# A table of attention decays written with one transfer and without its rows of ones, and its steps placed anew in a planned order

## The chip, the core and the metric

One core of a Trainium2 chip runs the whole program. Times are device microseconds of one execution. The core has five engines that run their own instruction lists side by side: PE (TensorE; its weight loads are listed apart as PEld), DVE (VectorE), ACT (ScalarE), POOL (GpSimd) and SP (SyncE, which here issues nearly every transfer between DRAM and the core's memory). An engine takes its instructions strictly in the order of its list, and an instruction waits until the steps that it needs have ended.

## The reference

Three stages follow each other: causal attention whose scores carry a decay, then two MLPs on the 2304 tokens (4 batches of 576) of width 512.

```python
# q, k, v: (4, 8, 576, 64), s: (4, 8, 576)
cum = np.cumsum(np.maximum(s, 0.0), axis=-1)
bias = -(cum[:, :, :, None] - cum[:, :, None, :])
scores = np.matmul(q, k.transpose(0, 1, 3, 2)) / np.sqrt(D)
scores = np.where(causal, -1e9, scores + np.minimum(bias, 0.0))
attn = softmax(scores)                       # + 1e-9 in the sum
x = (attn @ v) as 2304 tokens x 512
g = s1 * np.maximum(x @ w_in, 0.0) ** 2 + b1     # w_in 512 x 2048
x = g @ w_out                                # w_out 2048 x 512
h = np.maximum(np.maximum(x @ w1, x @ w2), x @ w3)   # 512 x 768 each
return h @ w_out2                            # 768 x 512
```

The bias at query i and key j is `cum[j] - cum[i]`. Only its part that depends on the key has to stand in the scores (what depends on the query alone leaves the softmax as it is), and the kernel takes off a middle value of the query's chunk to keep the numbers small.

## The kernel before

**Jobs.** Attention runs in jobs of two heads of one batch. The four pairs of batch 0 are split into an A job (queries 0 to 319) and a B job (queries 320 to 575) each: jobs 0 to 7. The twelve pairs of the other batches are one W job each: jobs 8 to 19. For each job PE makes the scores in units of up to 128 queries (`qk` L521/L523, `qk_set` L531 for W jobs), DVE adds the mask and takes the row's least value (`least` L542), ACT takes the exponentials into `pp` (`expo` L548), PE transposes `pp` into a bank `pt` (`turn_p` L589), ACT or DVE copies the bank into the job's buffer `pt` (`copy_p`, which is recorded under `copy`, L235 on ACT and L239 on DVE), and PE multiplies with v (`av` L608). Beside that DVE inverts the rows' sums (`inverse` L555/L556), POOL splits them into two parts (`rr`, L562/L563), PE turns and spreads them (L567, L579), and DVE multiplies the job's result with them (`x`, L613), which is split into `xhi` and `xlo` and stored (L625).

**Two ways to the decay.** For jobs 0 to 7 PE multiplies a one-hot tile `oh` (L511) with the tile `dd`, five pieces that hold the decays of every head as a rounded part and a rest: `df` is the decay (DVE), `dh` its rounding (ACT, L498), `dd` the rounding or the rest (DVE, L502). For the W jobs the scores of one head are made from two static tiles `set` [128, 4, 576] whose slots are QA, KA (rounded q and k over what is left of them) and KB, QB (the same crosswise). In rows 0 to 63 of KB and QB stand zeros but for rows 0 to 3: two rows of decays against rows of ones, in KB rows 0 and 1 are decays and 2 and 3 ones, in QB the other way round. So one product over all 128 rows adds the decay to the score. `clear_set` zeroes those rows once (POOL memset, L449), `round_set` (ACT, L471) and `rest_set` (POOL, recorded in `minus`, L242) fill the rest for each head, and `decay_set` brings the four rows of the head (L481).

**The table.** Those rows come from a table of all 32 heads in DRAM, `dm_d`. It is made in `dm` [32, 4, 576]: row 0 is the rounded `cum` (ACT, L430), row 1 what is left (DVE, L432), rows 2 and 3 the middle values of the chunks (DVE, L435/L437). `save_d` (L439 to L442) writes it with four transfers: two of `dm` and two that spread the constant `ones`, so that `dm_d` has for each head two blocks of four rows, one for KB and one for QB.

**What shares memory.** `dm` lies in the buffer of the second static set. `s4`, which holds `cum`, `ones` and `dh`, and `df` lie in buffers of the later `pt` tiles: the half-size `pt` of jobs 0 to 3 are cut out of the same two. So the first `copy_p` of a job must not start before the last `dd` is made, and before the change not before the table is saved either:

```python
over += [("dd", NC - 1), ("save_d",)]        # L766
```

**The weights.** Meanwhile a part of the first MLP's weights, `wa_in` and `wa_out`, is converted from a wider format in 16 pieces of 128x512, 8 of `w_in` and 8 of `w_out` (the rest follows in smaller side pieces): a load by SP (L271), a step on ACT (L275), four to six on DVE (L278 to L286), a rounding copy on ACT or DVE (L235, L239), a subtraction and an addition on DVE or POOL (L242, L290). The buffers `wg`, `stage` and `wst` hold a piece on its way. Two of these buffers are the `pt` buffers of the first W jobs: the first `copy_p` of a W job waits until all pieces are through (L765).

**The order.** The steps of this first half are not written in order. Each is handed to a planner with `add(name, engine, cost, priority, needs, ...)`; a step may name two engines with a cost for each. The planner (class `Plan`) simulates the engines by those costs: it takes the step that can begin first, and of steps within 0.03 of that the one with the lowest priority number, and in the order in which it has taken them they are written into the program. So a changed cost, priority or need can move any step on any engine. SP's transfers are ordered by it too.

Of the kernel before, what the change touches and what calls it, by code (L numbers as in the profile page):

```python
# [8 lines left out]
F32 = mybir.dt.float32  # L9
# [24 lines left out]
SET_AT = -10.0  # L34
# [159 lines left out]
def fused_kernel(ctx, tc, q, k, v, s, w_in, w_out, ms, mb, w1, w2, w3, w_fin, out,  # L194
                 f_split=8):
    nc = tc.nc
    B, H, S = s.shape
# [8 lines left out]
    NC = (S + P - 1) // P  # L206
# [118 lines left out]
    NH = B * H  # L325
# [95 lines left out]
    QA, KA, KB, QB = range(4)  # L421
    made = {}
    dm = atp.tile([NH, 4, S], F32R, name="dm", tag="set1")
    dmf = dm.bitcast(F32)
    dm_d = dram.tile([NH, 2, 4, S], F32, name="dm_d")

# [12 lines left out]
    def save_d():  # L439
        for z in range(2):  # L440
            nc.sync.dma_start(dm_d[:, z, 2 * z:2 * z + 2], dmf[:, 2 * z:2 * z + 2])
            nc.sync.dma_start(dm_d[:, 1 - z, 2 * z:2 * z + 2], ones[:NH].unsqueeze(1).to_broadcast([NH, 2, S]))  # L442

# [3 lines left out]
    def clear_set(z):  # L447
        made[z] = atp.tile([P, 4, S], F32R, name="set", tag=f"set{z}")
        nc.gpsimd.memset(made[z][:D, KB:].bitcast(F32), 0.0)  # L449

    def load_sb():
# [28 lines left out]
    def decay_set(job, j):  # L480
        nc.sync.dma_start(hs_[job.n, j][0:4, KB:].bitcast(F32), dm_d[2 * job.p + j].rearrange("t r n -> r t n"))  # L481

# [202 lines left out]
    for x, e in enumerate(("ACT", "DVE", "DVE", "DVE")):  # L685
        add(("dm", x), e, act(S) if e == "ACT" else dve(S), 8.0 + x, [("pre", "DVE")] + [("dm", y) for y in range(x)], decays, x, att=True)
    add(("save_d",), "SP", (4, 16), 8.0, [("dm", x) for x in range(4)], save_d, att=True)
    for z in range(2):
        add(("set", z), "Pool", 0.9, 20.0, [("save_d",)], clear_set, z, att=True)
    jobs = [Job(n, n % NP, "AB"[n // NP]) if n < 2 * NP else Job(n, n - NP, "W") for n in range((B + 1) * NP)]  # L690
    t0 = 0.0
    qk_key = lambda n, u, j: ("qk", n, u) if n < 2 * NP else ("qk", n, u, j)
    for job in jobs:
# [18 lines left out]
        if pairs:  # L712
            for key, when, m in (("q", Q_LOAD, job.q1 - job.q0), ("k", K_LOAD, job.keys)):
                add((key, n), "SP", (2, m), t0 + when, [] if key == "q" else [("q", n)], load_qk, job, key, take=[("raw", [("qk", n, u) for u in units])] if key == "q" else [], **a)
            add(("oh", n), "Pool", 0.3, t0 + TURN, [("qk", n - 2, u) for u in range(6)], one_hot, job, **a)
        else:
            for j in range(2):
                th = t0 + j * period / 2
                add(("q", n, j), "SP", (2, 2 * S), th + Q_LOAD, [], load_both, job, j, take=[("raw", [("rest", n, j), ("again", n, j)])], **a)
                add(("round", n, j), "ACT", act(2 * S), th + SET_AT, [("q", n, j)] + [("set", z) for z in range(2)], round_set, job, j, take=[("hs", [("qk", n, u, j) for u in units])], **a)  # L720
                add(("decay", n, j), "SP", (2, 16), th + SET_AT + 1, [("round", n, j), ("save_d",)], decay_set, job, j, **a)
                add(("rest", n, j), "Pool", pool_(2 * S), th + SET_AT + 1, [("round", n, j)], rest_set, job, j, **a)
                add(("again", n, j), {"Pool": pool_norm(S), "ACT": act(S)}, 0, th + SET_AT + 1.5, [("round", n, j)], again_set, job, j, **a)
# [30 lines left out]
        for z, (u, j) in enumerate(turns):  # L754
# [8 lines left out]
                if x == 0:  # L763
                    over = [("after", ("copy_p", n - 1, jobs[n - 1].units[-1], j))] if n else []
                    if 2 * NP <= n < 2 * NP + 3:  # L765
                        over += [("w", "a", z, 8) for z in range(16)] + [("av", 2 * NP - 1 - z, g) for z in range(2) for g in jobs[2 * NP - 1].groups]  # L766
                    over += [("dd", NC - 1), ("save_d",)]
                    take = [("ph" if n < 2 * NP else "p", [("av", n, g) for g in job.groups])]
# [428 lines left out]
```

## Time and profile before

| | |
|---|---|
| timed runs | 936.35, 941.95, 943.08 us; median 941.95 |
| profiled execution | 936.99 us, its span 935.2 us, mean granted clock of PE 0.991 |
| PE busy | 904.8 us (97% of the span), 5872 instructions |
| DVE busy | 518.1 us (55%) |
| ACT busy | 448.0 us (48%) |
| POOL busy | 243.9 us (26%) |

The span is the time that the profile shows; the execution's own time has a little more around it. A share over the whole span is a mean over stages with different limits: the attention and the first MLP overlap in the first third or so, the second MLP takes the rest. So the table says that PE fills the end, and nothing of what sets the start; for that the stretches have to be read apart.

In the rows further down, "out<-in" are the program's names, a size like 128x320 is partitions by elements, "x4" is a number of instructions, and brackets at the end of a row give the idle time of the engine just before it and what ended it. L12 is line 12 of the kernel before. In the new program some lines stand one further up or down (L548 is L549 there, L498 is L499, L449 is L447 and L448, L625 is L626).

### The profile page before, as it was taken

The numbers are of one execution on the slowest core, as the hardware profiler recorded it, in microseconds if no ns is written. First come the engines' busy times: TensorE is split into PE (matmuls) and PEld (weight loads), VectorE is DVE, ScalarE is ACT, GpSimd is POOL, SyncE is SP. The second block draws the span as 40 slices with busy tenths as digits, with TensorE's granted clock in tenths as the row PEclk, the third lists the DMA queues.
The fourth block names the chain that finished last, engine by engine and source line by source line (L and its number), as shares of the span: only waits on it lengthen the run. The fifth ranks groups of instructions, "written<-read, shape, count | busy, mean of one in ns | idle before, by whom it ended". The sixth has DMA issues, their size and how long they took to land.

```text
span 935.2 us, 16309 instructions
## 1 busy us (share of the span) xinstructions
PE 904.8 (97%) x5872; PEld 850.8 (91%) x5872; DVE 518.1 (55%) x1327; ACT 448.0 (48%) x1158; POOL 243.9 (26%) x286
## 2 busy tenths in 40 slices
PE   4899899999999999999999999999999999999997
PEld 3677789988898999999999999999999999999997
DVE  8798978877887312226687578578521213121221
ACT  4788699999977623324344335334221212121111
POOL 3344457655644233223233123210000000000000
PEclk8799999999999999999999999999999999999999
DMA  7455466675654003803334333433110202010000
GB/s 231 149 154 187 147 198 190 202 229 166 193 183 147 20 29 127 316 29 124 119 91 129 120 101 127 144 119 105 51 66 1 68 1 68 1 51 1 23 12 34
DMA packets 72497, 104.11 MB, mean 111 GB/s; under 512 B 7392, under 2 KB 48096, under 8 KB 72416
## 3 DMA queue, kind: packets, MB, share of 16 engines
q1 hardware_dynamic: 72320, 102.92, 34.9%
q8 instruction: 46, 0.75, 0.3%
q14 instruction: 35, 0.29, 0.1%
q10 hardware_dynamic: 96, 0.15, 0.0%
HBM read 75.19 MB, written 27.85 MB: 110 GB/s over the span
## 4 chain that ended last, share of the span: by engine, by line
PE 82%; DMA 6%; DVE 5%; ACT 4%; SPq 2%; issue 1%; POOL 1%; POOLq 0%; ACTq 0%; DVEq 0%
PE mm L246 23%; PE mm L248 23%; PE mm L247 23%; PE pt L589 4%; PE px L608 4%; PE ps L531 3%; PE ps L521 1%; DMA xs<-x_d 1%; DMA stage<-in_moe_w_in_dram 1%; DVE pp L542 1%; DMA raw<-in_k_dram 1%; ACT pt L235 1%; PE pr L579 1%; POOL ga L242 1%; DMA wb_in<-wb_d 1%
## 5 line engine op out<-in xcount | busy, mean ns | idle before, releaser
L246 PE MATMUL mm<-yh,wt 128*128 128x384 f32 x432 | 146.4, 339 | 0.0
L248 PE MATMUL mm<-yh,wt 128*128 128x384 f32 x432 | 146.3, 339 | 0.0
L247 PE MATMUL mm<-yl,wt 128*128 128x384 f32 x432 | 146.3, 339 | 0.0
L1101 DVE TENSOR_TENSOR u<-mm,u 128x384 f32<-128x384 f32 x72 | 40.1, 556 | 185.2 <-PE mm L248 185.2
L965 ACT ACTIVATE g<-g 128x384 f32<-128x384 f32 (+2 forms) x112 | 53.5, 477 | 146.1 <-DVE g L961 145.9
L589 PE MATMUL pt<-ident,pp 128*128 128x128 f32 x480 | 79.0, 280 | 15.9 <-ACT pt L235 12.5
L548 ACT ACTIVATE pp<-pp,mn 128x192 f32<-128x192 f32 (+4 forms) x160 | 88.8, 559 | 2.7 <-DVE mn L542 2.5
L242 POOL TENSOR_TENSOR gbl<-g,gbh 128x384 fp32r<-128x384 f32 x48 | 51.1, 1065 | 145.2 <-ACT gbh L235 134.5
L1105 ACT ACTIVATE hh<-u 128x384 fp32r<-128x384 f32 x36 | 18.9, 525 | 134.7 <-DVE u L1101 134.7
L246 PEld LDWEIGHTS mm<-yh,wt 128*128 128x128 f32 x432 | 81.2, 188 | 1.3
L247 PEld LDWEIGHTS mm<-yl,wt 128*128 128x128 f32 x432 | 81.2, 188 | 1.3
L248 PEld LDWEIGHTS mm<-yh,wt 128*128 128x128 f32 x432 | 81.2, 188 | 0.0
L242 POOL TENSOR_TENSOR set<-raw,set 64x1152 fp32r<-64x1152 f32 x24 | 65.1, 2712 | 61.4 <-ACT set L471 55.9
L246 PE MATMUL mm<-xhi,wa_in 128*128 128x320 f32 (+1 forms) x256 | 79.8, 312 | 1.3 <-DVE ya L1016 1.3
L961 DVE TENSOR_SCALAR g<-mm 128x384 f32<-128x384 f32 (+2 forms) x112 | 55.4, 495 | 45.0 <-PE mm L248 38.8
L246 PE MATMUL mm<-ga,wa_out 128*128 128x320 f32 (+2 forms) x256 | 79.8, 312 | 0.1
L248 PE MATMUL mm<-ga,wa_out 128*128 128x320 f32 (+2 forms) x256 | 76.2, 298 | 2.7 <-DVE wa_out L290 2.7
L589 PEld LDWEIGHTS pt<-ident,pp 128*128 128x128 f32 x480 | 56.1, 142 | 24.7 <-ACT pt L235 14.3
L235 ACT ACTIVATE pt<-pt 128x256 f32<-128x256 f32 (+3 forms) x181 | 72.4, 427 | 10.8 <-PE pt L589 8.9
L247 PE MATMUL mm<-ga,wa_out 128*128 128x320 f32 (+2 forms) x256 | 76.1, 297 | 0.8 <-POOL ga L242 0.8
L242 POOL TENSOR_TENSOR ga<-g,ga 128x320 fp32r<-128x320 f32 (+1 forms) x64 | 54.0, 845 | 87.4 <-ACT ga L235 85.2
L247 PE MATMUL mm<-xlo,wa_in 128*128 128x320 f32 (+1 forms) x256 | 75.8, 296 | 0.2 <-POOL xlo L242 0.2
(170 smaller groups left out, 2290.7 us busy)
## 6 DMA issues: line engine op xcount, KB each, us to landing
wst<-in_moe_w_dram SPq DMA_DIRECT2D x24, 384.0 KB, 3.7
raw<-in_q_dram SPq DMA_DIRECT2D x24, 288.0 KB, 3.6
raw<-in_k_dram SPq DMA_DIRECT2D x24, 288.0 KB, 3.8
wb_d<-wbs SPq DMA_DIRECT2D x21, 256.0 KB, 3.0
xs<-x_d SPq DMA_DIRECT2D x24, 192.0 KB, 3.7
y<-y_d SPq DMA_DIRECT2D x24, 192.0 KB
y_d<-y SPq DMA_DIRECT2D x24, 192.0 KB
yt<-y_d SPq DMA_DIRECT2D x24, 192.0 KB, 2.8
```

The source lines that it names most:

```text
L235: nc.scalar.activation(dst, src, AF.Copy, scale=1.0 if scale is None else scale)
L242: ENGINES[on].tensor_tensor(dst, a, b, op=ALU.subtract)
L246: nc.tensor.matmul(ps, lhs[0], rhs[0], start=first, stop=False)
L247: nc.tensor.matmul(ps, lhs[0], rhs[1], start=False, stop=False)
L248: nc.tensor.matmul(ps, lhs[1], rhs[0], start=False, stop=last)
L531: nc.tensor.matmul(ps[:, :k1 - k0], t[:, a, QS[i]:QS[i] + P], t[:, b, k0:k1], start=x == 0, stop=x == 1)
L548: nc.scalar.activation(p[:n, :w], p[:n, :w], AF.Exp, bias=mns[job.n, j][:n, i:i + 1], scale=-1.0, accum_out=sums[job.n % 2][:n, j, i:i + 1])
L589: nc.tensor.transpose(pt[:, c - c0, :], pp[j][i][:, c * P:(c + 1) * P], ident)
L608: nc.tensor.matmul(px_[job.n][hf][j * D:(j + 1) * D, a0 - h0:h1 - h0], vn[job.n % 2][:, c, j, :], columns(job, pr["p", job.n, j], c, c + 1 ...
L961: nc.vector.tensor_scalar(st["g", f], st["u", f][:, :n], 0.0, None, op0=ALU.max)
L965: nc.scalar.activation(st["g", f], st["g", f], AF.Square)
L1101: nc.vector.tensor_tensor(us[t0, f], us[t0, f, i][:, :N3], us[t0, f], op=ALU.max)
```

## The change

The table in DRAM holds four rows for each head and no ones; one transfer writes it. `clear_set` now sets rows 0 to 3 of KB and QB to one (a second memset on POOL), and `decay_set` brings two rows into KB (rows 0 and 1) and two into QB (rows 2 and 3) by two transfers for each head in place of one; the rows of ones are never written again. In the plan, the table's first two steps get an earlier place and its last two a later one, the save a later one, costs are fitted to the new steps, and the first `copy_p` of a job needs the second step of the table (the last that reads `cum`) in place of the save.

```diff
-    dm_d = dram.tile([NH, 2, 4, S], F32, name="dm_d")
+    dm_d = dram.tile([NH, 4, S], F32, name="dm_d")
...
     def save_d():
-        for z in range(2):
-            nc.sync.dma_start(dm_d[:, z, 2 * z:2 * z + 2], dmf[:, 2 * z:2 * z + 2])
-            nc.sync.dma_start(dm_d[:, 1 - z, 2 * z:2 * z + 2], ones[:NH].unsqueeze(1).to_broadcast([NH, 2, S]))
+        nc.sync.dma_start(dm_d, dmf)
...
     def clear_set(z):
         made[z] = atp.tile([P, 4, S], F32R, name="set", tag=f"set{z}")
         nc.gpsimd.memset(made[z][:D, KB:].bitcast(F32), 0.0)
+        nc.gpsimd.memset(made[z][:4, KB:].bitcast(F32), 1.0)
...
     def decay_set(job, j):
-        nc.sync.dma_start(hs_[job.n, j][0:4, KB:].bitcast(F32), dm_d[2 * job.p + j].rearrange("t r n -> r t n"))
+        t = hs_[job.n, j].bitcast(F32)
+        for a, z in ((0, KB), (2, QB)):
+            nc.sync.dma_start(t[a:a + 2, z], dm_d[2 * job.p + j, a:a + 2])
...
     for x, e in enumerate(("ACT", "DVE", "DVE", "DVE")):
-        add(("dm", x), e, act(S) if e == "ACT" else dve(S), 8.0 + x, [("pre", "DVE")] + [("dm", y) for y in range(x)], decays, x, att=True)
-    add(("save_d",), "SP", (4, 16), 8.0, [("dm", x) for x in range(4)], save_d, att=True)
+        add(("dm", x), e, act(S) if e == "ACT" else dve(S), (-1.0 if x < 2 else 12.0) + x, [("pre", "DVE")] + [("dm", y) for y in range(x)], decays, x, att=True)
+    add(("save_d",), "SP", (1, 72), 14.0, [("dm", x) for x in range(4)], save_d, att=True)
     for z in range(2):
-        add(("set", z), "Pool", 0.9, 20.0, [("save_d",)], clear_set, z, att=True)
+        add(("set", z), "Pool", 2.2, 20.0, [("save_d",)], clear_set, z, att=True)
...
-                add(("decay", n, j), "SP", (2, 16), th + SET_AT + 1, [("round", n, j), ("save_d",)], decay_set, job, j, **a)
+                add(("decay", n, j), "SP", (2, 18), th + SET_AT + 1, [("round", n, j), ("save_d",)], decay_set, job, j, **a)
...
-                    over += [("dd", NC - 1), ("save_d",)]
+                    over += [("dd", NC - 1), ("dm", 1)]
```

The plan comes out anew on all engines. Three places of it matter here.

ACT, from the last of the decays' roundings (`s_110<-df 128x576`, the `dh` that the last `dd` needs; its tile is named after the memory) to the first copies `pt` of job 0. Before:

```order
L498 ACTIVATE s_110<-df 128x576
L548 ACTIVATE pp_1_151,sums_144<-pp_1_151,mn 128x192
L548 ACTIVATE pp_1_156,sums_144<-pp_1_156,mn 128x192
L548 ACTIVATE pp_2_152,sums_144<-pp_2_152,mn 128x320
L275 ACTIVATE wg<-wg 128x512 x2
L548 ACTIVATE pp_2_157,sums_144<-pp_2_157,mn 128x320
L275 ACTIVATE stage<-stage 128x512 x2
L235 ACTIVATE wa_in<-wg 128x512
L275 ACTIVATE stage<-wst 128x512
L275 ACTIVATE wg<-wg 128x512
L235 ACTIVATE wa_in<-wg 128x512
L235 ACTIVATE wa_in<-stage 128x512 x2
```

Behind the last of these rows come the two copies `pt<-pt 128x64`. Now, with what each waits for (a number behind an engine's name is of no matter here, DMAHW7 is the landing of a transfer):

```order
L499 ACTIVATE s_110<-df 128x448 [waits DVE_49,Activation_49]
L275 ACTIVATE wg<-wg 128x512 [waits DMAHW7_49]
L549 ACTIVATE pp_0_150,sums_144<-pp_0_150,mn 64x64 [waits DVE_49]
L549 ACTIVATE pp_0_155,sums_144<-pp_0_155,mn 64x64 [waits DVE_49]
L499 ACTIVATE s_110<-df 128x576 [waits DVE_49]
L549 ACTIVATE pp_1_151,sums_144<-pp_1_151,mn 128x192 [waits DVE_49]
L549 ACTIVATE pp_1_156,sums_144<-pp_1_156,mn 128x192 [waits DVE_49]
L235 ACTIVATE wa_in<-wg 128x512 [waits DVE_49]
L235 ACTIVATE pt<-pt 128x64 [waits DVE_49,PE_49]
L235 ACTIVATE pt<-pt 128x64 [waits PE_49]
L549 ACTIVATE pp_2_152,sums_144<-pp_2_152,mn 128x320
```

The first copy now stands behind four exponentials, one rounding and one step of a weight piece (the second piece, `wg`), which itself has moved ahead of the exponentials; before, six exponentials, six weight steps and four roundings stood ahead of it.

POOL, around the memsets of the static sets. Before, both stood together, ahead of `xlo` of job 0:

```order
L449 MEMSET set 64x1152 x2
L242 TENSOR_TENSOR stage<-stage,wa_in 128x512
L511 CAST oh<-rows 128x128
L290 TENSOR_TENSOR wa_in<-stage 128x512
L242 TENSOR_TENSOR xlo<-x_0_457,xhi 128x320
L562 CAST rr<-rs 128x2x3
```

Now (DMAHW5 is the save of the table):

```order
L242 TENSOR_TENSOR xlo<-x_0_417,xhi 128x320 [waits Activation_49]
L512 CAST oh<-rows 128x128 [waits PE_49]
L447 MEMSET set 64x1152
L448 MEMSET set 4x1152 [waits Pool_49]
L242 TENSOR_TENSOR xlo<-x_0_542,xhi 128x320 [waits Activation_49]
L447 MEMSET set 64x1152 [waits DMAHW5_49]
L448 MEMSET set 4x1152 [waits Pool_49]
L563 CAST rr<-rs 128x2x3 [waits DVE_49]
L564 TENSOR_TENSOR rr<-rs,rr 128x2x3 [waits Pool_49]
```

The memsets have moved behind `xlo` of job 0, the second of them stands behind the save and ahead of `rr` of job 2, and the subtraction and the addition of a `stage` piece have left POOL (three others of the conversion leave it later, all for DVE).

SP, where the weights of `w_out` (`stage<-in_moe_w_out_dram`) and the table's save stand among the attention's loads. Before, from the save on:

```order
L441 DMA dm_d<-dm 32x1152
L442 DMA dm_d<-s_110 32x2x576
L271 DMA wg<-in_moe_w_in_dram 128x512
L487 DMA vn_115<-in_v_dram 128x2x128
L489 DMA vn_115<-in_v_dram 64x128
L461 DMA raw<-in_q_dram 64x320 x2
L271 DMA stage<-in_moe_w_out_dram 128x512 x2
L625 DMA x_d<-x_0_457 128x320
```

Now the save stands behind the result of job 0 (`x_d<-x_0_417`), and the first load of `w_out` further down, behind the keys of job 5:

```order
L626 DMA x_d<-x_0_417 128x320 [waits DMAHW4_49,DVE_49]
L440 DMA dm_d<-dm 32x2304 [waits DMAHW5_49,DVE_49,Activation_49]
L488 DMA vn_116<-in_v_dram 128x2x128 [waits DMAHW6_49,PE_49]
...
L460 DMA raw<-in_k_dram 64x576 [waits DMAHW1_49]
L460 DMA raw<-in_k_dram 64x576 [waits DMAHW2_49]
L271 DMA stage<-in_moe_w_out_dram 128x512 [waits DMAHW3_49,DVE_49]
L488 DMA vn_116<-in_v_dram 128x4x128 [waits DMAHW4_49,PE_49,Pool_49]
```

So the loads of `w_out` come later among the attention's own loads: the second stands behind the next job's q and k, the third behind the first q and k of a W job.

## Rows read from the trace of the kernel before

**Rows 1.** Windows: start:end length, busy of PE PEld DVE ACT POOL, PEclk, DMA, GB/s.

```profile
10.50:34.00 23.50, 9.35 (x47) 6.06 (x48) 19.57 (x55) 13.62 (x39) 5.99 (x6) 0.64 0.66 206
34.00:55.00 21.00, 20.81 (x158) 14.87 (x157) 19.83 (x67) 19.57 (x69) 8.29 (x14) 1.00 0.53 160
55.00:107.20 52.20, 49.22 (x362) 39.44 (x361) 47.11 (x121) 40.59 (x99) 24.17 (x27) 1.00 0.58 175
107.20:266.00 158.80, 156.79 (x1257) 142.06 (x1257) 127.27 (x459) 151.78 (x451) 94.73 (x92) 1.00 0.62 191
...
366.00:935.20 569.20, 563.33 (x3223) 549.35 (x3221) 249.70 (x476) 162.87 (x346) 66.56 (x72) 1.00 0.25 82
```

**Rows 2.** Timeline of PE: start us, length us, line, operation [idle before <-releaser].

```profile
27.07 1.54 PE L589 MATMUL pt<-ident,pp 128*128 128x128 f32 x6 [11.76 <-ACT pt L235]
```

**Rows 3.** Timeline of ACT.

```profile
11.42 0.33 ACT L548 ACTIVATE pp<-pp,mn 64x64 f32<-64x64 f32 x1
...
13.54 0.55 ACT L548 ACTIVATE pp<-pp,mn 128x320 f32<-128x320 f32 x1
14.08 0.65 ACT L275 ACTIVATE wg<-wg 128x512 f32<-128x512 f32 x1
...
26.82 0.85 ACT L235 ACTIVATE pt<-pt 128x64 f32<-128x64 f32 x4
...
107.21 1.37 ACT L235 ACTIVATE pt<-pt 128x64 f32<-128x64 f32 x4 [0.68 <-DVE wa_out L290]
```

**Rows 4.** Timeline of DVE.

```profile
12.94 0.80 DVE L502 SCALAR_TENSOR_TENSOR dd<-s,lower,df 128x576 fp32r<-128x576 f32 x1
...
29.42 0.21 DVE L542 CUSTOM_DVE_ANT_0 pp<-late_keys,ps 64x64 f32<-64x64 f32 x1 [2.83 <-PE ps L523]
...
36.02 0.49 DVE L613 TENSOR_TENSOR x<-px,rb 128x320 f32<-128x320 f32 x1
...
105.89 1.29 DVE L290 TENSOR_TENSOR wa_out<-stage 128x512 fp32r<-128x512 f32 x2
```

**Rows 5.** DVE's groups, 30 to 108 us: operation xcount | busy us, mean ns | idle.

```profile
L239 DVE COPY pt<-pt 128x512 f32<-128x512 f32 x2 | 1.4, 688 | 0.6 <-PE pt L589 0.6
L242 DVE TENSOR_TENSOR wg<-wg,wa_in 128x512 f32<-128x512 f32 x2 | 1.4, 677 | 0.0
...
L239 DVE CAST rt<-pr 128x128 fp32r<-128x128 f32 x2 | 0.6, 288 | 0.9 <-PE pr L567 0.9
```

**Rows 6.** An issue on SP; transfers (KB, us to landing); two rows of POOL.

```profile
8.36 0.58 SPq L271 DMA_DIRECT2D wg<-in_moe_w_in_dram  x1
...
raw<-in_q_dram SPq DMA_DIRECT2D x8, 80.0 KB, 2.4
...
wst<-in_moe_w_dram SPq DMA_DIRECT2D x24, 384.0 KB, 3.7
...
dm_d<-dm SPq DMA_DIRECT2D x2, 144.0 KB, 6.0
...
25.85 1.05 POOL L449 MEMSET set<- 64x1152 f32 x1 [6.30 <-DVE wg L286]
...
43.13 0.19 POOL L562 CAST rr<-rs 128x6 fp32r<-128x6 f32 x1 [2.83 <-DVE rs L556]
```

**Rows 7.** The set loads (ns min/median/max, first to last start) and POOL's first `rest`.

```profile
L481 SPq DMA_DIRECT2D set<-dm_d x24: 268/319/467, 81.4 to 301.7; - x24
...
82.51 3.13 POOL L242 TENSOR_TENSOR set<-raw,set 64x1152 fp32r<-64x1152 f32 x1 [0.34 <-POOL ga L242]
```

**Rows 8.** Timeline of SP's transfer issues: start us, length us.

```profile
36.83 0.99 SPq L271 DMA_DIRECT2D stage<-in_moe_w_out_dram  x2
...
49.00 1.89 SPq L461 DMA_DIRECT2D raw<-in_k_dram  x2
...
76.72 0.42 SPq L467 DMA_DIRECT2D raw<-in_k_dram  x1
...
96.08 0.34 SPq L271 DMA_DIRECT2D stage<-in_moe_w_out_dram  x1
```

## Prediction

> **What bounds the kernel now.** I read the stretches first, then PE's waits, then ACT and DVE in the first 40 us, then the place where the attention's first half hands over to its second.
>
> The stretches [rows 1] show three regimes. From 366 us to the end PE is busy 563.33 of 569.20 us: whatever happens earlier reaches the end only as a shift of that block. From 107.2 to 266 us ACT is busy 151.78 of 158.80 us and is the bound; DVE (127.27) follows. Before 107.2 us DVE is the fullest: 19.83 of 21.00 us, then 47.11 of 52.20. The hole lies between 10.5 and 34 us: of 23.50 us PE fills 9.35, ACT 13.62, but DVE 19.57. Counted on ACT the hole is 9.88 us, counted on DVE only 3.93.
>
> PE's longest wait is 11.76 us, ended at 27.07 by ACT's copies `pt`, which begin at 26.82 [rows 2, 3]. Their inputs had long been there; the plan puts them behind the save of the table, and so behind ACT's steps on weight pieces that land late.
>
> The handover: the first `pt` copy of a W job starts at 107.21, after 0.68 us of waiting for DVE's last `wa_out` additions (105.89 and 1.29 us for two) [rows 3, 4]. It goes into a buffer in which weight pieces were converted, so no W copy can start before the sixteen pieces are through. DVE's work up to there is the clock of the front part, and how much of the 11 us survives it is what has to be predicted.
>
> **The start, moved.** In the new order ACT's first `pt` copy stands behind four exponentials, the first step of weight piece 2 and a rounding of piece 1. Piece 2 is issued at 8.36 and takes 0.58 to issue [rows 6]; ACT runs its step at 14.08 without a wait [rows 3]. The landing is not shown: not after 14.08, and not before 8.94 + 2.4, the quickest median of a load [rows 6]. I take 8.94 + 3.7, that of weight pieces, the nearest row: 12.6. Then 0.6 for the step, 2.1 for the exponentials with `dh` between (11.42 to 13.54 now) and as much for the rounding, which has the step's shape, as for the step [rows 3] put the copy at 15.9, **10.9 us** before 26.82. That is the gain if nothing else were late. DVE is late next. Up to the handover, on DVE:
>
> 1. The wait of 2.83 us at 29.42, for scores behind the copies [rows 4], goes. New: `dd` needs `dh`, which now stands behind piece 2. `dd` starts 1.5 us after the first exponential now (12.94 and 11.42) [rows 3, 4], so at 13.2 + 1.5 = 14.7 in the new order; what stands ahead of it on DVE is what stands there now but for one longer conversion step, so I let it end at 13.2, a little after 12.94. So 1.5 us of waiting come. **-1.3** (-2.8 if the piece lands at 11.3, 0 if at 14.1).
> 2. Five additions of the conversion leave POOL for DVE at 0.68 each: +3.4. In return DVE gives ACT two large `pt` copies of 0.69 and two `rt` copies of 0.29: -2.0 [rows 5]. ACT takes them where it is busy 40.59 of 52.20 us [rows 1], so they cost nothing there; without that cover 2.0. **+1.4** (0.4, if DVE gains 1 us by less disturbance from POOL, to 3.4).
> 3. The second `set` memset on POOL now waits for the table's one save, since the table lies in that set's buffer. Behind it on POOL stands `rr` of job 2, and behind what needs that, on PE's queue, the scores of job 4. `x` of job 0 comes at 36.02 now, so at 25 [rows 4]; the table's last step stands some 4 us of DVE work behind it (sixteen rows of the new order, at 0.2 to 0.5 us each [rows 4]), so the save goes out at about 29. It has 288 KB: 3.7 us as a weight piece, 6.0 as half the table took [rows 6], so it lands between 32.7 and 35. Two memsets follow: 1.05 us [rows 6], and the four-row one, which the trace does not show; the nearest row is again 1.05 (as long, fewer rows), the other bound 0.2. POOL is through between 34 and 37; `rr` is wanted at 43.13 - 10.9 = 32.2 [rows 6]. The stall is 2 to 5 us, but DVE meets it only when the conversions that stand ahead of job 4's scores run out: **+1.0** (0 to 5).
> 4. Between 55 and 107.2 us DVE waits 5.09 us. With the attention ahead of it there is work at hand more often; I let the share fall to that of 34 to 55 us (1.17 of 21.00), so 2.9 of 52.2: **-2.2** [rows 1] (-5.1 to +2).
> 5. `x` of job 7 and two side pieces come ahead of the handover and cost before it what they save behind: 0, within 1 us.
>
> Sum: -1.3 + 1.4 + 1.0 - 2.2 = -1.1 us at the handover. Behind it the same work stands on a saturated ACT, so the shift is carried to the end.
>
> **The rest of the edit.** Four saves become one, off any path. Each of 24 set loads becomes two: one more SP issue of 0.32 us, 7.7 us in all between 81 and 302 us [rows 7]. The cover: SP issued the first at 81.4, and POOL's `rest` on that set, which the scores need as well, ran from 82.51 to 85.64 [rows 7]; a part that lands half a microsecond later stays hidden. Taken as 0; without the cover 7.7. The Trainium skill, page "DMA: Bandwidth & Descriptors", section "Rules for kernel authors", asks to coalesce many small transfers into a large one, since below 64 KB one pays mostly overhead. This part of the edit goes against that; by the rule the sum would be worse by the uncovered price. The trace has borne it out in issue time alone.
>
> The sum is made against the profiled execution, 936.99 us (span 935.2): 935.9. The median of the three timed runs is 941.95, 5.0 us above it, within 936.35 to 943.08; on its scale the sum gives 940.8. A new median may lie anywhere between the two: **938**.
>
> **Rivals.**
> - *The whole hole counts.* If DVE packs its weight work between attention steps and its waits vanish, the shift is the 10.9 us of the first copy: 926 us (928.5 on the middle scale). For it: ACT, the bound from 107 us on, loses 9.88 us in the hole. Against: DVE loses 3.93 there and gets five additions more. Chance 0.17.
> - *Slower: the second half of the weights comes too late.* The eight `wa_out` loads go out between 36.83 and 96.08 [rows 8], and the last additions end at 107.18: 70 us for eight. In the new order the first load stands behind the keys of job 5 (49.00 now [rows 8], so about 38 to 40) and the third behind the first keys of a W job (76.72 now, so about 66). If the chain of load, ACT and DVE for a piece sets the pace and not DVE's work, the handover comes at 111 to 115, 4 to 8 us later: 941 to 945 us (943.5 to 947.5). It decides when the last six pieces take over 41 us from 66. Against: the last load went out at 96.08 and its piece was through 11 us later, side by side with another, so pieces overlap. Chance 0.15.
> - *The start is not freed*, because the copies wait for something of the table after all: 937 (939.5). Against: the first copy's waits in the new order name DVE and PE and no transfer. Chance 0.03.
> - *Set loads uncovered*: 935.9 + 7.7 = 943.6 (946). Chance 0.04.
>
> The forecast's own case has 0.61; its items reach from 929 to 945 together, 931 to 942 if not all fall on one side. The range that leaves out no more than 2 in 10 is **927 to 945**. 1% is 9.4 us, about what a measurement of this kernel can tell from no change. Faster by that needs nearly the whole of the first rival, slower more than the second's price: faster 0.14, same 0.80, slower 0.06.
>
> **What would show it.** The first `pt` copy at 15 to 17 us and no PE wait over 4 us after it. DVE busy about 1.5 us longer before the first W copy, its waits 2 to 4 us shorter, and that copy at 104 to 108. A wait of POOL for the save ahead of the second memset, with `rr` of job 2 behind it. ACT 95% busy from there for some 159 us. If the first W copy comes before 100 us, the first rival holds and items 2 to 4 are too dear; after 110, the second; if it comes at 106 and the end is elsewhere, the carrying behind the handover is wrong.

## The result, and the profile after

The changed kernel takes **947.68 us** (median of 12 executions, 943.77 to 949.82) against 941.89 (936.12 to 944.06) for the kernel before beside it: a ratio of **1.0064**, 95% interval 1.0041 to 1.0087. It is slower by 5.8 us where 938 was forecast and 927 to 945 was the range. The profiled execution took 948.05 us (span 946.2) against 936.99 (935.2), so the two traces lie 11 us apart, more than the medians: the profiled execution of before is one of its shortest.

The stretches of the changed kernel, cut as in [rows 1] but for the third, which again ends at the first `pt` copy of a W job:

```profile
10.50:34.00 23.50, 19.71 (x111) 13.18 (x108) 18.13 (x64) 18.50 (x63) 2.88 (x7) 0.71 0.73 216
34.00:55.00 21.00, 19.84 (x139) 13.85 (x138) 17.08 (x55) 17.48 (x54) 10.09 (x15) 1.00 0.49 143
55.00:115.90 60.90, 49.01 (x323) 38.17 (x322) 53.09 (x127) 40.82 (x100) 20.56 (x25) 0.87 0.48 148
115.90:266.00 150.10, 146.13 (x1169) 130.95 (x1169) 122.68 (x422) 137.78 (x410) 88.39 (x87) 1.00 0.60 187
366.00:946.20 580.20, 574.57 (x3319) 560.76 (x3317) 250.91 (x483) 169.52 (x362) 73.61 (x82) 1.00 0.25 81
```

From 10.5 us to that copy DVE is busy 88.30 of 105.4 us (before 86.51 of 96.7). Its work grew by 1.8 us, its waits by 6.9, and the two make up the 8.7 us by which the copy is late. The waits are the clear part of it: another execution of the kernel before (e14, copy at 107.20) has 88.91 us of DVE's work and 7.79 of waits, so that the work varies within one kernel by more than 1.8 us. Against [rows 1] the waits grew in each of the three stretches: 3.93 to 5.37, 1.17 to 3.92, 5.09 to 7.81. The hole of PE is filled (19.71 for 9.35 us), and another has opened behind 55 us. ACT in the timeline, the first copy of job 0, the last step before the first W copy that waited long, and that copy:

```profile
16.16 0.31 ACT L235 ACTIVATE pt<-pt 128x64 f32<-128x64 f32 x2
...
113.75 0.44 ACT L275 ACTIVATE wb<-wb 128x256 f32<-128x256 f32 x1 [2.35 <-DMA wb<-in_moe_w_in_dram]
...
115.88 1.33 ACT L235 ACTIVATE pt<-pt 128x64 f32<-128x64 f32 x4
```

So the start came as computed (15.9 forecast, 16.16 measured, 26.82 before [rows 3]) and the lead of 10.7 us has turned into a delay of 8.7. The last exponential of a job, read from ACT's timeline, shows where it went:

| last exponential ends, us | job 1 | job 3 | job 4 | job 6 | job 7 |
|---|---|---|---|---|---|
| before | 37.0 | 50.2 | 58.0 | 78.5 | 90.1 |
| changed | 27.1 | 41.0 | 52.9 | 77.2 | 92.8 |

The lead is down to 1.3 us at job 6 and lost at job 7, and all that time the weights are behind: the fifth piece's last addition comes at 54.58 instead of 35.52, the eleventh at 98.19 instead of 73.23. SP's loads of `w_out` and the first side piece behind them, then DVE where it waited or was held up:

```profile
71.50 0.38 SPq L271 DMA_DIRECT2D wst<-in_moe_w_out_dram  x1
...
99.31 0.54 SPq L271 DMA_DIRECT2D wst<-in_moe_w_out_dram  x1
...
107.26 0.33 SPq L271 DMA_DIRECT2D stage<-in_moe_w_out_dram  x1
110.67 0.33 SPq L271 DMA_DIRECT2D wb<-in_moe_w_in_dram  x1
```

```profile
25.05 0.49 DVE L543 CUSTOM_DVE_ANT_0 pp<-late_keys,ps 128x320 f32<-128x320 f32 x1 [2.32 <-PE ps L524]
...
30.34 0.35 DVE L543 CUSTOM_DVE_ANT_0 pp<-late_keys,ps 128x192 f32<-128x192 f32 x1 [1.48 <-PE ps L524]
...
37.36 1.77 DVE L556 TENSOR_SCALAR rs<-sums 128x6 f32<-128x6 f32 x1
...
49.39 0.49 DVE L614 TENSOR_TENSOR x<-px,rb 128x320 f32<-128x320 f32 x1 [2.16 <-DMA x_d<-x]
...
87.82 2.88 DVE L280 SCALAR_TENSOR_TENSOR stage<-stage 128x512 int32<-128x512 int32 x1
...
95.21 0.45 DVE L543 CUSTOM_DVE_ANT_0 pp<-late_keys,ps 128x288 f32<-128x288 f32 x1 [1.91 <-PE ps L532]
...
105.00 0.43 DVE L278 TENSOR_SCALAR stage<-stage 128x512 int32<-128x512 int32 x1 [1.85 <-ACT stage L275]
...
106.55 0.68 DVE L290 TENSOR_TENSOR wa_out<-stage 128x512 fp32r<-128x512 f32 x1
...
116.84 0.68 DVE L290 TENSOR_TENSOR wa_out<-stage 128x512 fp32r<-128x512 f32 x1
```

The third load of `w_out` goes out at 71.50 and the last piece is through at 117.52. The load at 107.26 waits until a buffer is free: it goes out 0.03 us after the addition of an earlier piece ends (106.55 and 0.68). The side piece, which stands ahead of the W copy on ACT, goes out behind it, and ACT waits 2.35 us for that piece. It waited as long for one before:

```profile
104.81 0.44 ACT L275 ACTIVATE wb<-wb 128x256 f32<-128x256 f32 x1 [2.32 <-DMA wb<-in_moe_w_in_dram]
```

There the copy then waited 0.68 us more for the last additions [rows 3]. Now it doesn't wait for the last piece: it begins at 115.88, 1.0 us ahead of that piece's addition. That no W copy can start before all sixteen pieces are through held in the trace of before and doesn't hold here.

PE's side of it, how long it waited for whom (total, times, longest) from 60 to 120 us, and stretches of PE (columns as above), the last four at half clock:

```profile
PE mm L248 <- DVE wa_out L290: 7.6, 3, 5.0
PE ps L532 <- DVE mn L543: 3.5, 1, 3.5
```

```profile
0.00:34.00 34.00, 27.93 (x157) 21.16 (x157) 23.86 (x79) 21.80 (x67) 9.42 (x37) 0.80 0.70 201
34.00:120.00 86.00, 72.57 (x479) 55.27 (x478) 74.27 (x195) 61.45 (x158) 31.18 (x40) 0.90 0.46 141
...
14.30:24.50 10.20, 9.27 (x45) 5.88 (x44) 7.37 (x23) 8.86 (x31) 0.39 (x2) 0.50 0.79 252
28.00:31.20 3.20, 3.20 (x15) 2.11 (x16) 1.72 (x10) 2.70 (x10) 1.44 (x3) 0.50 0.71 239
93.00:96.20 3.20, 3.20 (x15) 2.54 (x17) 1.22 (x6) 3.14 (x11) 1.12 (x3) 0.50 0.74 225
103.10:116.80 13.70, 7.26 (x26) 6.87 (x27) 11.44 (x25) 5.77 (x13) 0.00 (x0) 0.50 0.38 135
```

The same two long stretches of the kernel before, and its one stretch at half clock:

```profile
0.00:34.00 34.00, 17.32 (x99) 13.57 (x100) 25.84 (x71) 17.40 (x44) 12.44 (x36) 0.75 0.65 194
34.00:120.00 86.00, 82.83 (x610) 66.45 (x611) 79.03 (x230) 72.47 (x205) 40.27 (x48) 1.00 0.54 164
...
16.50:33.60 17.10, 6.53 (x33) 4.40 (x33) 13.17 (x33) 8.72 (x24) 5.50 (x5) 0.50 0.56 177
```

Up to 120 us PE stands idle 6.1 + 13.4 = 19.5 us now and 16.7 + 3.2 = 19.9 before. **The idle time has only moved.** In these two traces the clock differs too: before, PE was busy 6.53 us while it ran at 1.2 GHz; now it does some 23 us of its work at that level.

But that is a difference of two executions, not of the two kernels. The trace of before has a mean granted clock of 0.991. The 129 executions of the kernel before that ran beside the experiments have 0.984 in the mean, and so have the 12 of the changed kernel. At a mean clock of 0.984 the kernel before takes 940.9 us (mean of 16 executions) and the changed one 947.8 (of 4). So the half clock widens the gap between the two traces; it doesn't make the loss in the medians.

### The profile page after: what moved, and what is told of

The parts are those of the page before. It is cut to its first block, busy times and chain, and to the rows that moved or that the text cites. A ratio compares the mean times of both kernels' runs of the same rounds, so it can differ in the third digit from the quotient of the medians.

```text
span 946.2 us, 16340 instructions
## 1 busy us (share of the span) xinstructions
PE 915.2 (97%) x5872; PEld 856.2 (90%) x5872; DVE 521.6 (55%) x1329; ACT 449.5 (48%) x1160; POOL 238.7 (25%) x284
## 4 chain that ended last, share of the span: by engine, by line
PE 81%; DMA 7%; ACT 5%; DVE 4%; issue 1%; SPq 1%; POOL 1%; ACTq 0%; DVEq 0%; POOLq 0%
PE mm L246 22%; PE mm L248 22%; PE mm L247 22%; PE pt L590 5%; PE px L609 4%; PE ps L532 3%; ACT pp L549 1%; PE ps L522 1%; DMA x_d<-x 1%; DMA xs<-x_d 1%; ACT pt L235 1%; DMA wbs<-in_moe_w_in_dram 1%; DMA wb_d<-wb 1%; PE pr L580 1%; DMA wb<-in_moe_w_in_dram 1%
## 5 line engine op out<-in xcount | busy, mean ns | idle before, releaser
L590 PE MATMUL pt<-ident,pp 128*128 128x128 f32 x480 | 81.5, 285 | 7.1 <-ACT pp L549 4.5
L248 PE MATMUL mm<-ga,wa_out 128*128 128x320 f32 (+2 forms) x256 | 77.7, 304 | 7.6 <-DVE wa_out L290 7.6
L246 PE MATMUL mm<-ga,wa_out 128*128 128x320 f32 (+2 forms) x256 | 81.1, 317 | 0.9 <-ACT wa_out L235 0.9
L246 PE MATMUL mm<-xhi,wa_in 128*128 128x320 f32 (+1 forms) x256 | 79.3, 310 | 0.3 <-ACT xhi L235 0.2
L247 PE MATMUL mm<-ga,wa_out 128*128 128x320 f32 (+2 forms) x256 | 77.2, 301 | 0.6 <-POOL ga L242 0.4
L248 PE MATMUL mm<-xhi,wa_in 128*128 128x320 f32 (+1 forms) x256 | 75.8, 296 | 0.0
L235 ACT ACTIVATE pt<-pt 128x64 f32<-128x64 f32 (+3 forms) x183 | 73.2, 426 | 4.8 <-PE pt L590 3.7
```

Source lines behind the costliest of these rows:

```text
L235: nc.scalar.activation(dst, src, AF.Copy, scale=1.0 if scale is None else scale)
L246: nc.tensor.matmul(ps, lhs[0], rhs[0], start=first, stop=False)
L247: nc.tensor.matmul(ps, lhs[0], rhs[1], start=False, stop=False)
L248: nc.tensor.matmul(ps, lhs[1], rhs[0], start=False, stop=last)
L590: nc.tensor.transpose(pt[:, c - c0, :], pp[j][i][:, c * P:(c + 1) * P], ident)
```

## The experiments

Ratios are to the kernel before on the same chip, from 12 executions (6 and 7 in e7 and e5); medians of different rows can come from different chips, so rows are compared by their ratios. "W copy" is the first `pt` copy of a W job in the profiled execution, whose own time stands beside it; that one is not always near the median (e3's and e4's are the longest of their twelve).

| run | median us | ratio | 95% interval | W copy (execution) |
|---|---|---|---|---|
| e1 data part, old order | 941.19 | 0.9978 | 0.9954 to 1.0001 | 110.39 (942.06) |
| e2 changed, weights early | 940.60 | 0.9999 | 0.9981 to 1.0017 | 111.65 (940.84) |
| e3 changed, memsets later | 944.11 | 1.0020 | 1.0002 to 1.0037 | 109.98 (946.74) |
| e4 changed, clock held | 942.46 | 1.0013 | 0.9996 to 1.0030 | 114.99 (947.16) |
| e5 changed again | 946.51 | 1.0060 | 1.0036 to 1.0084 | 114.86 (946.87) |
| e6 old order, weights early | 937.16 | 0.9958 | 0.9938 to 0.9979 | 104.01 (934.55) |
| e7 old order, 220 transposes | 951.04 | 1.0112 | 1.0086 to 1.0139 | 117.85 (948.88) |
| e8 changed, all three | 938.84 | 0.9984 | 0.9967 to 1.0002 | 106.13 (937.00) |
| e9 changed, memsets and clock | 942.21 | 1.0021 | 1.0001 to 1.0040 | 115.11 (942.71) |
| e10 changed, additions on POOL | 943.05 | 1.0035 | 1.0010 to 1.0059 | 109.72 (946.17) |
| e11 e9 with weights early | 937.48 | 0.9972 | 0.9956 to 0.9989 | 109.78 (936.88) |
| e12 old order, 95 transposes | 938.86 | 0.9986 | 0.9967 to 1.0004 | 106.07 (939.04) |
| e13 changed, less DVE work | 941.53 | 1.0009 | 0.9988 to 1.0030 | 111.89 (944.15) |
| e14 before again | 941.18 | 0.9990 | 0.9967 to 1.0013 | 107.20 (936.06) |
| e15 e1 with weights early | 936.97 | 0.9957 | 0.9934 to 0.9979 | 102.84 (933.13) |
| e16 e15 with clock held | 935.10 | 0.9946 | 0.9924 to 0.9969 | 104.49 (934.52) |

**e1.** The new data in the old order.

```diff
-    add(("dm", x), e, ..., (-1.0 if x < 2 else 12.0) + x, ...)
+    add(("dm", x), e, ..., 8.0 + x, ...)
-    add(("save_d",), "SP", (1, 72), 14.0, ...)
+    add(("save_d",), "SP", (4, 16), 8.0, ...)
-        add(("set", z), "Pool", 2.2, 20.0, ...)
+        add(("set", z), "Pool", 0.9, 20.0, ...)
-                add(("decay", n, j), "SP", (2, 18), ...)
+                add(("decay", n, j), "SP", (2, 16), ...)
-                    over += [("dd", NC - 1), ("dm", 1)]
+                    over += [("dd", NC - 1), ("save_d",)]
```

> The new table, the one save, the memset of ones and the two set loads for each head, with the old places, costs and needs in the plan, so that all other steps keep the order of the kernel before. Late weights (the second half of the weights' pieces reaches the first W job too late in the new order): as the kernel before, 940 to 943 us, first W copy at about 107. Slow start (the half clock and the memsets behind the save hold up the first 50 us of the new order): the same, since that start is not here. Dear data (a second set load for each head, more memsets): the kernel before plus 4 to 8 us, 946 to 950.

No slower than before. The second set load of each head and the memsets of ones cost nothing that can be measured: the whole loss lies in the order. Its trace says the same at a like clock: 18.09 us of PE's work at half clock from 11.4 to 42.1 us and 6.70 more from 110.4 to 117.1, as much as in the changed kernel's trace, and yet 942.06 us for 948.05.

**e2.** Weight pieces wanted earlier in the new order.

```diff
-W_2 = 29.041
+W_2 = 19.041
```

> The changed kernel with the conversion of pieces 4 to 15 wanted 10 us earlier in the plan (one number, W_2, 29.041 to 19.041), as much as the attention's start has moved. Late weights: the first W copy comes 4 to 9 us earlier than 115.9, at 107 to 112, and the time falls by about as much, to 939 to 944 us. Slow start: the conversion only changes places with attention, first W copy at 114 to 117, 946 to 949 us. Dear data: no change, 946 to 949.

Level with before, 0.6% under the changed kernel (e5), and the copy at 111.65, both as late weights had it. PE's waits for `wa_out` are gone; from 60 to 120 us its longest wait is now for the attention:

```profile
PE pt L590 <- ACT pp L549: 6.3, 4, 2.6
```

**e3.** The memsets of both sets, which wait for the save, behind `rr` of job 3.

```diff
         for t, key, engine, f in plan.order():
+            if key in (("set", 0), ("set", 1)):
+                held.append(f)
+                continue
             f()
+            if key == ("split_r", 3):
+                for g in held:
+                    g()
```

> The changed kernel with both sets' memsets (and so POOL's wait for the save) put behind the rr steps of job 3, everything else in its order. Slow start: the memsets no longer stand before rr of job 2 nor beside DVE's sums at 37 us, so what follows them comes 1.5 to 3 us earlier, and the time falls to 945 to 946 us. Late weights: up to 2 us earlier at 50 us, but the last pieces wait for their buffers, so the first W copy comes 0 to 1 us earlier, 947 to 948 us. Dear data: as slow start at most, since the memsets stay.

0.4% under e5, in the direction of a slow start and more than its 945 to 946 us; the W copy came 5 us earlier, which no theory had. POOL in the changed kernel, then DVE's same step `rs` in e3:

```profile
37.24 0.86 POOL L242 TENSOR_TENSOR xlo<-x,xhi 128x320 fp32r<-128x320 f32 x1 [0.36 <-ACT xhi L235]
38.04 1.05 POOL L447 MEMSET set<- 64x1152 f32 x1
39.16 1.05 POOL L448 MEMSET set<- 4x1152 f32 x1
40.16 0.61 POOL L563 CAST rr<-rs 128x6 fp32r<-128x6 f32 x1
```

```profile
35.03 0.57 DVE L556 TENSOR_SCALAR rs<-sums 128x6 f32<-128x6 f32 x1
```

With `xlo` and then a memset beside it, `rs` takes 1.77 us (37.36 to 39.13) and ends with the first memset; in e3, beside `xlo` alone, 0.57. So the memsets held up not only `rr` on POOL (0.8 us behind the inverse of `rs`) but DVE itself, by 1.2 us. That the gain of e3 is all theirs is not shown: its trace has no half clock from 28.0 to 31.2 and from 93.0 to 96.2 either.

**e4.** Transposes of the identity in PE's first gaps.

```diff
         pt = bank("pt").rearrange("p (c n) -> p c n", n=P)
+        for _ in range({(0, 0, 0): 24, (0, 1, 0): 14, (0, 1, 1): 6, (0, 2, 0): 4, (1, 2, 0): 12}.get((job.n, u, j), 0)):
+            nc.tensor.transpose(pt[:, 0, :], ident, ident)
```

> The changed kernel with 60 more transposes of the identity on PE (into the bank that the real ones then overwrite), in its gaps between 12.6 and 16.5 us and at 27 us, so that its granted clock stays at full speed there; the rest in its order. If the clock stays up: slow start says that PE's scores come 2 to 4 us earlier at 34 us and the time falls by 2 to 3 us, to 945 to 946; late weights says that the first W copy moves by less than 1 us and the time stays at 947 to 948. If the clock falls all the same, nothing changes.

The clock stayed at 1.00 where it had been 0.50 from 14.3 to 24.5, and the ratio to the kernel before fell by 0.5%, more than forecast. The mean clock of the executions rose from 0.984 to 0.992. The profiled execution, the longest of the twelve and the one with the lowest mean clock (0.989), doesn't show the gain: there the clock falls at 27.4 us after all, PE waits for a load of keys at 25.2, and the last 12 transposes delay the scores of job 2.

**e5.** The changed kernel once more.

> The changed kernel itself, beside the other runs of this call. Any theory: 0.5 to 0.9% slower than the kernel before on the same chip, 946 to 949 us; if it comes out level with the kernel before, the gains read from the earlier variants were those of a chip.

Its loss is there again, and its trace repeats the first to about 1 us.

**e6.** The one number of e2 on the kernel before.

> The kernel before with the same one number of the plan moved (weight pieces 4 to 15 wanted 10 us earlier). Late weights as a fault of the new order alone: the old order converts in time, so 0 to 2 us of gain, 939 to 942. If the conversion bounds the old order as much, it gains the 4 to 7 us that the new order gained from it, 934 to 937.

Between the two: -0.42% (0.2 either way). The conversion bounds the old order too; that it does so less than the new one, where the same number gave 0.61% (0.3 either way, from e2 and e5), is not shown.

**e7, e12.** Transposes in the hole of the kernel before, 220 and then 95.

```diff
+        for _ in range({(0, 1, 1): 220}.get((job.n, u, j), 0)):
+            nc.tensor.transpose(pt[:, 0, :], ident, ident)
```

> The kernel before with 220 more transposes of the identity on PE in its 11.8 us hole, so that the granted clock stays up there. If the half clock behind the hole costs the old order what it costs the new one (from 27 to 33 us of PE work at half speed, some 3 us), 937 to 939 us and a first W copy 2 to 3 us earlier; if DVE's work sets the old order's pace there, no change, 940 to 943.

```profile
15.63 24.24 PE L589 MATMUL pt<-ident 128*128 128x128 f32 x220 [1.13 <-DVE mn L542]
```

Mis-sized: one takes 0.110 us, and 220 in an 11.8 us hole had reckoned with half of it, so they ran on to 39.87 and pushed the attention back by 13 us. It became another experiment: in the old order 13 us of delay at the start cost 10 us at the end.

> The kernel before with 95 instead of 220 transposes of the identity in its hole (10.5 us at 0.11 each, over before the copies at 27 us). If the half clock behind the hole costs the old order too: 937 to 939 us, first W copy 2 to 3 us earlier. If DVE's work sets the pace there: no change, 940 to 943.

With 95 the mean clock of the executions rises from 0.985 to 0.993 and the time falls by 0.14% (interval to +0.04): at most a little. In the profiled execution the transposes begin at half clock and take 12.40 us, to 27.08, so they end with the hole and not before it.

**e8, e9, e11.** Combinations on the changed kernel: e3's and e4's edits with the plan's numbers below (e8), e3's with fewer transposes (e9), that with e2's number (e11).

```diff
 # e8
-W_2 = 29.041
+W_2 = 18.041
-LATE_0 = 0.991
+LATE_0 = 0.5
 # e9, e11: the transposes
+        for _ in range({(0, 0, 0): 12, (0, 1, 0): 7, (0, 1, 1): 3, (0, 2, 0): 2}.get((job.n, u, j), 0)):
```

> The changed kernel with the three edits together: the pieces wanted 11 us earlier (and POOL taken for an addition where it is 0.5 rather than 0.99 us sooner), the sets' memsets behind rr of job 3, the 60 transposes that hold the clock. Late weights: the first W copy at 103 to 108 and 934 to 939 us. Slow start: each of the two edits on the start keeps its 3 to 4 us and the third adds little, 939 to 941. If all three remove the same wait, no better than the best alone, 940 to 942.

> The changed kernel with both edits on its start and none on the weights: the sets' memsets behind rr of job 3, and 24 transposes of the identity in PE's first gaps (0.11 us each by the run with 220 of them, so 2.6 us in all, none later than job 0). Slow start as the whole of the loss: the two gains add up (4 and 5 us), the time comes to 937 to 939 us, 0.3% under the kernel before. Late weights behind it: the gains overlap, 942 to 944 us, 0.1 to 0.3% over the kernel before, with the first W copy at 110 to 112.

> Both edits on the start and the weight pieces wanted 10 us earlier, on the changed kernel. Late weights and slow start as two losses: 935 to 938 us, first W copy at 104 to 107, level with or under the old order with early weights (937). If they remove the same wait: 940 to 942, as with early weights alone.

The gains overlap: e9 is no better than e3 or e4 alone, and its W copy (115.11) is later than the 110 to 112 forecast. With the weights early the start seems to count again: e11 is 0.27% under e2, with some 0.25 either way. It is 0.14% over e6, and e8, with all three edits, lies between e2 and e11; neither is clear of the intervals.

**e10.** The five steps of the conversion that had left POOL (three subtractions and two additions; the prediction calls all five additions) forced back to it.

```diff
+            if name == "a" and (z, i) in {(3, 7), (4, 8), (6, 8), (9, 7), (11, 7)}:
+                engine = {"Pool": pool_(n), "DVE": 1e6}
             add(("w", name, z, i), engine, cost, ...)
```

> The changed kernel with the same five additions of the weights' conversion on POOL that stood there before (the rest of the plan made anew round them). If the additions on DVE are what the new order lost (1.4 us of DVE work by the prediction), DVE is busy 3 us less up to the first W copy and the time falls by 1 to 3 us, to 944 to 946. If DVE's waits are the loss and not its work, no change or up to 2 us slower, 946 to 949, since POOL takes 2.5 us for what DVE does in 0.7.

0.25% under e5, within the two intervals, and the rest of the order moved with it: not settled.

**e13.** Two of DVE's steps of each `w_out` piece left out.

```diff
-        nc.vector.scalar_tensor_tensor(g, word(U32, 0), 2.0 ** -52, g, op0=ALU.mult, op1=ALU.mult)
+        if not short:
+            nc.vector.scalar_tensor_tensor(g, word(U32, 0), 2.0 ** -52, g, op0=ALU.mult, op1=ALU.mult)
...
-        minus(a, a, hi.bitcast(F32), on)
+        minus(lo if short else a, a, hi.bitcast(F32), on)
...
-        ENGINES[on].tensor_tensor(lo, a, g, op=ALU.add)
+        if not short:
+            ENGINES[on].tensor_tensor(lo, a, g, op=ALU.add)
```

> The changed kernel with two DVE steps (0.68 us each) left out of each of the eight w_out pieces, so 10.9 us of DVE work less before the first W copy; the low parts of these weights are then only what the rounding left of the first 24 bits. The order is otherwise the same. If DVE's work and the late pieces set the front part: first W copy 6 to 11 us earlier, at 105 to 109, PE's idle time between 80 and 117 us (11 us) falls below 5, and the time to 936 to 941 us. If PE's clock and the attention set it: first W copy 2 to 4 us earlier, 943 to 946.

0.5% under e5, at 941.53 us between the two forecasts, with the W copy at 111.89, 3 to 4 us earlier, as PE's clock and the attention had it. PE is busy 27.92 of the 37 us from 80 on, for 25.11 in the changed kernel. Its idle time there is 9.1 us, not below 5. Half of what was taken off DVE (10.9 us) reaches the end, so DVE's work is one bound of the front part and not the only one.

**e14.** 

> The kernel before once more, for another profiled execution. If the half clock makes the old order's own spread (936 to 944 us): an execution near 941 shows some 10 us more of PE work at half clock than the profiled one of 937 us. If not, the same stretch of 17 us as there.

The profiled execution took 936.06 us and repeats the first (half clock for the same 17 us). e1, in the same order, took 942.06 with this:

```profile
11.40:42.10 30.70, 18.09 (x82) 11.77 (x81) 23.53 (x68) 18.17 (x57) 11.44 (x13) 0.50 0.56 162
```

The two traces of 936 us, with 17 us at half clock, say nothing of the executions at 941, but the mean clock of every execution is on record. Of the 129 of the kernel before, the ten with the highest (0.989 to 0.991) took 935.0 to 940.8 us and the twelve with the lowest (0.979 and 0.980) 940.8 to 946.3. So a long execution of the old order goes with a lower clock. That the clock makes the time is not shown by that: e12 raised the clock further and gained 0.14%.

**e15, e16.** e1 with the weights early, and e16 with transposes in the hole as well.

```diff
-W_2 = 29.041
+W_2 = 19.041
 # e16
+        for _ in range({(0, 1, 1): 85}.get((job.n, u, j), 0)):
```

> The old order with the new table (as in the run with the data part alone) and the pieces wanted 10 us earlier. If the parts add up (-0.2% and -0.4%): 934 to 937 us. If the data part's -0.2% was chance: 937 to 938.

> The same with 85 transposes of the identity (9.4 us) in PE's hole, so that the clock is up when the copies come. If the half clock costs the old order 2 us: 932 to 935 us; if not, as without them, 934 to 938.

e16 is the shortest of all, 0.54% under the kernel before (0.31 to 0.76%); e15 alone 0.43%, so that the transposes' 0.11% lies within the intervals. From 80 to 117 us PE in e15 is busy 36.84 of 37 us.

## Why the prediction was wrong, point by point

**DVE's waits** are where the sum went wrong. Items 1, 3 and 4 together put them 2.5 us shorter; up to the first W copy they are 6.9 us longer (9.3 against e14's trace).

**The first copy** came where it was put, 16.16 for 15.9. That it would gain little was right too: PE's idle time up to 120 us is the same.

**Item 1 (-1.3)** failed. The wait of 2.83 us went and `dd` waited 1.06 for the 1.5 forecast, but waits of 2.32 and 1.48 us for scores stand in their place, and the stretch to 34 us has 1.4 us more of waiting than before. PE was at half clock before both (to 24.5, and from 28.0 to 31.2), and the prediction counted PE's hole and not the clock in it. That the clock makes these waits is not shown: e4's trace, at full clock to 27 us, has 6.06 us of waiting in that stretch for 5.37.

**Item 2 (+1.4)** can't be judged. DVE's work grew by 1.8, but between the two traces of the kernel before it differs by 2.4 (86.51 and 88.91), so that the figure fits is luck. Nor does e10 settle its worth in time.

**Item 3 (+1.0, up to 5)** was the right mechanism. `rr` of job 2 came 0.8 us behind the inverse of its `rs`, but 1.2 us more went on DVE, where the prediction looked for none. e3 is 0.4% under e5, not by the memsets alone as far as is known. The four-row memset takes 1.05 as taken. Of the 2.75 us by which DVE's waits from 34 to 55 us grew, 2.16 are one wait at 49.39, put down to a store of `x`, of which the prediction has nothing.

**Item 4 (-2.2)** is the step that failed outright: "With the attention ahead of it there is work at hand more often". Behind 55 us DVE waits 7.81 for 5.09 us (2.55 in e14's trace). With the attention served first, the pieces' loads wait behind it for their buffers, DVE meets products, scores and loads that are not there, and what it could have done meanwhile has not landed. That earlier weights take back the loss (e2) fits this.

**Item 5 (0)** is open. ACT's wait of 2.35 us for a side piece ahead of the W copy is no new one (2.32 before), but now nothing behind it covers it: the copy follows without waiting for the last additions.

**The rival that came true** is that of the late second half of the weights. Its point was 41 us from the third load; it took 46. Its price (943.5 to 947.5 on the scale of the runs) ended 0.2 us short of the median, and with a chance of 0.15 it was given too little: the row against it, that the last piece took 11 us, said nothing of three buffers that eight pieces share. But it need not be the whole: the number that brings the weights early takes back all of the loss here, and gains 0.42% in the old order too. Of the loss of 0.60% the differences of the runs would give 0.2 to weights that come later than the old order's, 0.27 to the start (e11 against e2: memsets and clock) and leave 0.14. Only the 0.27 is clear of its uncertainty, and barely. Shown is that the order makes the loss (e1), and that early weights, less DVE work, later memsets or a held clock each take back 0.4 to 0.6% of the time, with gains that overlap. How the loss divides among them stays open.

**Set loads uncovered (7.7 us)** is refuted by e1. The Trainium skill's rule to coalesce small transfers ("DMA: Bandwidth & Descriptors", "Rules for kernel authors") spoke against this part of the edit; here two transfers of two rows cost no time over one of eight that e1 can measure. The trace agrees with it in SP's issue time alone (0.65 us for the first pair, at 71.97, for 0.38 before).

**The carrying** behind the first W copy held in most runs (828.0 us to the end before, 830.3 after) and not in all: e11 has 825.3, e3 835.0. So that copy is a fair sign and no measure. What of PE's time behind it differs stays open.

## What to carry to other kernels

A hole in the timeline of the engine that bounds the end is worth only as much as the engine behind it can follow: count the idle time of the whole front part, not of the hole, and look what waits for a buffer once the order changes. When steps are moved ahead in a planned order, ask which steps give way, and move their due times too: here one number for the weights took back the whole loss, and gained 0.42% in the old order. And compare traces of executions with a like granted clock: one of the shortest executions of the kernel before, beside a usual one of the changed kernel, made the clock look like a part of the loss.

## What was not expected of the hardware

- A memset of 4 rows takes as long as one of 64 (1.05 us each, 1152 elements a row).
- A transpose of 128x128 in f32 on PE takes 0.110 us at full clock (220 in 24.24 us), and 220 of them in a row left the granted clock at 1.00.
- A DVE instruction of 0.16 us took 1.77 beside POOL's `xlo` and memset, and one of 0.68 us, with two inputs, took 2.88 beside POOL's `rest` (87.53 to 90.15). The Trainium skill ("SBUF — State Buffer", "Who interferes with whom") has a rule for both: the two engines share a pair of ports, which the one that comes first holds for its whole instruction. The trace agrees in the second place, where `rest` began first and DVE ended 0.55 us behind it. In the first it agrees in part: `rs` began behind `xlo` but ahead of the memset (37.36 and 38.04), and ended with the memset all the same. In both places DVE paid.
